# w_out in eight pieces, q of the first batch in whole rows, and 120 shifted priorities in a two-stage kernel that orders itself

## The chip, the cores and the metric

The kernel runs on one core of one Trainium2 chip. The metric is the device time of one execution in microseconds; the kernel before was run three times. A profile is one execution, with its own time.

## What is computed

Attention with random features on 8 batches of 8 heads, 576 tokens of 64 values each, followed by a feed-forward layer with a gate on the 4608 tokens that result. Cut to what matters:

```python
# stage 1, per batch and head; q, k, v: [8, 8, 576, 64], omega: [128, 64]
q_s, k_s = q / 64**0.25, k / 64**0.25
def phi(x):                              # [.., 576, 128]
    h = x @ omega.T - sum(x * x) / 2
    return exp(h - max(h)) / sqrt(128)   # the maximum over the 128 features
q_p, k_p = phi(q_s), phi(k_s)
kv = k_p.T @ v                           # [128, 64]
z = sum(k_p, over tokens)
attn = (q_p @ kv) / (q_p @ z + 1e-6)

# stage 2; x: [4608, 512] (batch and token, head and value), w_in: [512, 2048], w_out: [2048, 512]
h = x @ w_in
out = (h * clip(h + 3, 0, 6) / 6) @ w_out
```

Inputs and output are float32; the products run in bf16. Terms of phi(q) that are the same for all features of a token cancel in the quotient, so for q only the exponential of the projection is formed; for k each token's scale is the reciprocal of its largest exponential.

## The kernel before

**Tiling.** A batch has four pairs of heads (m = 0 to 3) and 576 tokens: 512 "main" tokens and 64 left over, which are set side by side for the two heads of a pair. Main tokens of one head lie in 128 partitions by 4. A "double" is 128 columns of a transposed tile: two heads' or two rows' 64 values. Every PSUM tile is one bank of eight (`ring`).

**Stage 1 of one batch** (`attention`, and inside it `pair`): k and q are transposed (names `Tk`, `Tq`; matmuls at L430, from batch 2 on DMA transposes), projected on omega (`K`, L652; `Q`, L669), and ScalarE takes the exponential (L658, L673). VectorE takes the maxima of k's features (L661, `mx`) and their reciprocals (`cc`), v is scaled by them (`vc`, L763; for the left tokens `vcl`, L692). `kv` (L776, L778) gathers the pair's product into one bank, a copy makes it bf16 (`kvz`), `num` (L804) multiplies it with q's exponentials, VectorE divides (L820, `xb`), and a transpose (`X`, L430 again) gives xT. The left tokens of all batches are gathered in xS and make a ninth block.

**Stage 2 of one block of 512 tokens**: `mm1` (L872; for block 0 `mm1_half`, L897) multiplies with w_in, 16 groups of 128 features; ScalarE and VectorE form the gate (L878, L880; L906, L908) into gT; `mm2` (L930) multiplies with w_out, 16 products into each of four tiles of 128 tokens; a copy and a store follow. Block 0 goes in two halves, A and B: for half A only 256 tokens of every head have to be through stage 1. Its mm2 tiles 0 and 1 need half A alone.

**Loads.** Batch 0's k, q and v come as float32 by the queues of SyncE (SP) and ScalarE, and are cast by engines. All weights, and k and q of later batches, are cast by the DMA itself and are issued by GpSimd (POOL); v stays float32. `FIRST` is the order of batch 0's loads: in the kernel before k, its left tokens, then `("q", 1)`, half A of q (`q_half(0)`: rows of tokens 0 to 255, four transfers of 128 KB in runs of 512 B), v, and `("q", 2)`, half B, which is issued when v's last transfer has landed (`QB_GATE`). `W_GATE` holds the four pieces of w_in back until half A's last transfer is in. Batch 1's k is issued when w_in's second piece is in, its q after the third, its v after the fourth; w_out after a transfer of batch 1's k; batch 2's loads after w_out's pieces 1, 2 and 3.

**What sets the order.** The program records every operation with its engine or engines, an estimated duration, what it reads and writes, and a priority (`prio`, mostly the batch or block in which it is due). `Prog.schedule` then plays the program through with those durations: each engine takes, among the operations that could start earliest, the one with the lowest priority; an operation with several possible engines goes to one of them; DMA queues share a modelled rate. What comes out is a fixed order for each engine, and `emit` writes it with the semaphore waits that the reads and writes need. On the chip each engine executes its list in that order. Where TensorE is idle in that play before 21 us, operations named `idle` (L467, `fill`) are put in: matmuls on a constant, whose results nobody reads.

Of the kernel before, what the change touches and what calls it, by code (L numbers as in the profile page):

```python
# [13 lines left out]
FIT = 0.1  # L14
IDLE_UNTIL = 21.0
EV0 = (("ACT","DVE"), ("ACT","DVE"), ("POOL","DVE"), {"k": ("POOL", "ACT", "DVE"), "q": ("POOL", "ACT","DVE")})


class Virt:
# [299 lines left out]
def _emit(nc, es, q, k, v, omega, w_in, w_out, out):  # L319
    B, H, S, D = q.shape  # L320
# [5 lines left out]
    NP = H // 2  # L326
# [5 lines left out]
    MAIN = 512  # L332
# [1 line left out]
    HALVES = [(0, 2), (2, 4)]  # L334
    SPLIT = 3
    LATE = 0.4
    FIRST = [("k", 1), ("k", 0), ("q", 1), ("v", 0), ("v", 1), ("q", 2), ("q", 0)]
    QB_GATE = [("v32", 1, 3)]
    REST = [("k", 1), ("k", 0), ("q", 1), ("q", 0), ("v", 0), ("v", 1)]
    W_GATE = [("q32", 1, 3, 0)] * 4  # L340
    alpha = float(D) ** -0.25
    PE_T, PE_X = 2, 2
    SPARE = 1
# [56 lines left out]
    G = Prog()  # L400
    op = G.op

    def mmt(n):
        return 0.003 + n / 2400.0
# [70 lines left out]
    def w_in_piece(i, gate):  # L475
# [3 lines left out]
           -8.6 + 0.05 * i, reads=gate, writes=[("wi", i)], group="dwi%d" % i, inc=16, lat=1.0, name="wi%d" % i,  # L479
           issue=0.85, packet=91.0)  # L480

    def w_out_piece(g, gate):
        op("POOL", 2.95, lambda E: E.dma_start(
            wo[:, 4 * g:4 * g + 4, :], w_out[512 * g:512 * g + 512, :].rearrange("(c p) e -> p c e", p=128)),
           -0.2 + 0.05 * g, reads=gate, writes=[("wo", g)], group="dwo%d" % g, inc=16, lat=1.0, name="wo%d" % g,
           issue=0.85, packet=91.0)

# [4 lines left out]
    def load(b, eng, gates):  # L492
        pb = b % 2
        halves = HALVES if b == 0 else [(0, NP)]
        turn_of = [0]

        def dma(part, dst, src, n, keys, gate, prio, run):
            cast = b > 0 and part[0] in "kq"
            e = "POOL" if cast else eng[turn_of[0]] if turn_of[0] < len(eng) else "SP"
            op(e, n * (0.74 if b == 0 else 0.8) * {1024: 1.0, 512: 1.1, 256: 1.5}[run] / 262144.0,  # L500
               lambda E: E.dma_start(dst, src), prio + 0.001 * turn_of[0], reads=gate + (free if cast else []), writes=keys,  # L501
               group="d" + part + ("c" if cast else "") + (str(pb) if b and part != "v" else ""), inc=16, lat=1.0,
               name="%s.%d" % (part, b), issue=0.85 if cast else 0.47, packet={1024: 50.0, 512: 36.0, 256: 18.0}[run])
            turn_of[0] += 1


        free = [("kb", 0, x) for x in range(NDC)] if b == 1 else []

        def landing(t, hh, m0, m1):

            if t == "v" or b == 0:
                return [(t + "32", hh, m) for m in range(m0, m1)]
            return [(t + "b", pb, 2 + 4 * m + 2 * hh + x) for m in range(m0, m1) for x in range(2)]

        base = {t: (b - 1) - {"k": 0.32, "q": 0.30, "v": 0.20}[t] if b else -9.5 for t in "kqv"}

        def mains(t, src, dst):
            for x, (m0, m1) in enumerate(halves):
                for hh in range(2):
                    first = 64 * hh if t != "q" else 0  # L520
                    d = dst[:].rearrange("p m (h r) d -> p m h (r d)", h=2) if t == "v" else mains_of(dst)
                    rows = src[b, 2 * m0 + hh:2 * m1 - 1 + hh:2, first:first + MAIN, :]
                    dma("%s%d%d" % (t, hh, x), d[:, m0:m1, hh, :], rows.rearrange("m (p r) d -> p m (r d)", r=4),
                        131072 * (m1 - m0), landing(t, hh, m0, m1), gates[t], base[t], 1024)

        def lefts_of(t, hh):
            return [(t + "b", pb, x, hh) for x in range(2)]

        def lefts(t, src, dst):
            if t == "q":  # L530
                for hh in range(2):
                    dma("ql%d" % hh, dst[64 * hh:64 * hh + 64, 0:NP, :],
                        src[b, hh:H:2, MAIN:S].rearrange("m s d -> s m d"), 65536, [("q32l", hh)] if b == 0 else lefts_of(t, hh),
                        gates[t], base[t], 256)
            else:
                sap = src[b].rearrange("(m h) s d -> m (h s) d", h=2)[:, MAIN:MAIN + 128, :]
                dma(t + "l", vl[pb][:, :, 0:D] if t == "v" else dst[:, 0:NP, :],
                    sap.rearrange("m x d -> x m d"), 131072, [("vl", pb)] if t == "v" else [("k32l", 0)] if b == 0 else lefts_of(t, 0),
                    gates[t], base[t], 256)

        def q_half(half):

            for m0, m1 in HALVES:
                for hh in range(2):
                    d = q32[:, NP:, :].rearrange("p (m h s r) d -> p m h s (r d)", h=2, s=2, r=2)
                    rows = q[0, 2 * m0 + hh:2 * m1 - 1 + hh:2, 256 * half:256 * half + 256, :]
                    dma("q%d%d%d" % (hh, m0, half), d[:, m0:m1, hh, half, :], rows.rearrange("m (p r) d -> p m (r d)", r=2),
                        65536 * (m1 - m0), [("q32", hh, m, half) for m in range(m0, m1)], QB_GATE if half else [], base["q"], 512)

        tensors = {"k": (k, KB[pb] if b else k32), "q": (q, QB[pb] if b else q32), "v": (v, v32)}  # L550
        for t, part in FIRST if b == 0 else REST:
            if t == "q" and b == 0 and part:
                q_half(part - 1)
            else:
                (mains if part else lefts)(t, *tensors[t])


    def attention(b):
# [10 lines left out]
        def main_keys(t, ms, hs=(0, 1)):  # L569
            return [(t + "32", hh, m) for m in ms for hh in hs]  # L570
# [45 lines left out]
        if b == 0:  # L616
# [7 lines left out]
            for s in range(2):  # L624
                for m0, m1 in HALVES:
                    nm = "%d%s" % (m0 // 2, "AB"[s])
                    dbl = every(m0, m1, s)
                    cast("q", nm, 512, pairs(qb)[:, 2 * m0:2 * m1, s, :], pairs(q32)[:, 2 * m0:2 * m1, s, :],
                         [k_ + (s,) for k_ in main_keys("q", range(m0, m1))], dbl, 0)
                    turns("q", nm, dbl, alts(qT, s, m0, m1), qb, 0)  # L630
            for t, src, cst, dst in (("k", k32, kb, kT), ("q", q32, qb, qT)):
                late = 0 if t == "k" else LATE
# [283 lines left out]
    def mm2(blk, tc):  # L916
# [5 lines left out]
        for ci, (c0, c1) in enumerate(cols):  # L922
            w = c1 - c0
            vo = Virt(ring)
            for g in range(4):
                t = (blk + 1) + (4 * tc + g + 0.5) / 16.0 + 0.5 * ci

                def e(E, g=g, vo=vo, c0=c0, c1=c1):
                    for f in range(4 * g, 4 * g + 4):
                        ins = E.matmul(ring.t[vo.slot][:, 0:c1 - c0], gT[gu][:, f, 128 * tc:128 * tc + 128], wo[:, f, c0:c1],  # L930
                                       start=(f == 0), stop=(f == NF - 1))
                    return ins

                op("PE", 4 * mmt(w), e, t, reads=[("gT", gu, f, tc // 2) for f in range(4 * g, 4 * g + 4)] +
                   [("wo", g)],
                   writes=[vo], alloc=[vo] if g == 0 else [], lat=0.25,
                   spare=(3 if tc > 1 else 0) if blk == 0 and g == 0 else 0, name="mm2.%d.%d" % (blk, tc))
            keys = [("osb", ou, x) for x in ((0, 1) if w == 512 else (ci,))]
            op(EV_O, both(w), evac(lambda c0=c0, c1=c1: osb[ou][:, c0:c1], lambda vo=vo, w=w: ring.t[vo.slot][:, 0:w]),
               t - 0.05, reads=[vo], writes=keys, name="oev.%d.%d" % (blk, tc))  # L940
            if blk < 8:
                rows = out[blk * S:blk * S + MAIN, :]
                dsts = [(0, 128, rows[256 * (tc // 2):256 * (tc // 2) + 256, :].rearrange("(p r) e -> r p e", r=2)[tc % 2] if blk == 0 else
                         rows.rearrange("(p r) e -> r p e", r=4)[tc])]
            else:
                dsts = [(64 * i, 64, out[(2 * tc + i) * S + MAIN:(2 * tc + i) * S + S, c0:c1]) for i in range(2)]
            for p0, np_, dst in dsts:
# [6 lines left out]
    for b in range(B):  # L954
        if b == 0:
            load(0, ("SP", "ACT", "SP", "ACT"), {t: [] for t in "kqv"})
            for i in range(len(WI)):
                w_in_piece(i, [W_GATE[i]])
        elif b == 1:
            load(1, (), {"k": [("wi", 1)], "q": [("wi", 2)], "v": [("wi", 3)]})  # L960
            for g, key in enumerate((("kb", 1, 16),)*4):
                w_out_piece(g, [key])
        elif b == 2:
            load(2, (), {"k": [("wo", 1)], "q": [("wo", 2)], "v": [("wo", 3)]})
        else:
            load(b, (), {"k": [("m1", b - 2, 6)], "q": [("m1", b - 2, 9)], "v": [("m1", b - 2, 15)]})
        if b == 0:
# [21 lines left out]

    G.by_path([o for o in G.ops if o.name == "mm1.0B.0"], -0.3, 0.02)  # L990
    G.by_path([o for o in G.ops if o.name == "mm1.0A.0"], -1.0, 0.02)
    G.schedule()
    engs = {"PE": nc.tensor, "ACT": nc.scalar, "DVE": nc.vector, "POOL": nc.gpsimd, "SP": nc.sync}
    blkx = es.enter_context(nc.Block())
# [35 lines left out]
```

The softmax here doesn't subtract the row's maximum and nothing guards it: scores larger than these inputs give would overflow.

## Time and profile before

| | us |
|---|---|
| median of three runs | 325.93 (325.68 to 326.29) |
| the profiled execution's own time | 325.93 |
| its span, first to last instruction | 324.1 |
| TensorE busy (share of the span) | 315.3 (97%) |
| VectorE, ScalarE, GpSimd busy | 211.3, 188.6, 75.1 |
| granted TensorE clock, mean | 0.999 |

Busy time of TensorE by stretch of the span, where what is missing is idle: 16.39 of the first 18.00 us, 21.66 of the 24.00 to 42, 15.74 of the 16.00 to 58, 41.74 of the 42.00 to 100. Matmuls overlap and their ends are modelled, so a busy stretch can hold small gaps, and the fill matmuls count as busy.

The first loads and the POOL queue, from the views of single transfers: k's last transfer (the left tokens) lands 4.4 us after its issue at 2.17; q's half A 4.1 to 4.3 us after issues from 2.68 to 4.25; v's last at 12.01; w_in's four pieces are issued from 8.69 to 11.88 and take 6.0 to 14.5 us; w_out's four are issued from 28.55 to 31.53 and take 10.1 to 15.4.

In the page, "L430" is the line of every TensorE transpose, so k, q and x are told apart by the tile after the arrow (`p<-ident,qb` is a transpose of q). A bracket after a row names the idle time of the engine before the row and whose end ended it.

### The profile page before, as it was taken

Reading aid. Unit: us, or ns where it says so; the run is one execution under the profiler, and the core shown is the slowest. Engines: PE = TensorE matmul, PEld = TensorE weight load, DVE = VectorE, ACT = ScalarE, POOL = GpSimd, SP = SyncE. Lnnn points to the kernel's source line nnn. Section 1 sums busy time; section 2 is a strip of 40 time slices with the busy share of each in tenths; the row PEclk is TensorE's granted clock in tenths of the full one; section 3 lists DMA queues with packets and bytes.
Section 4 is the critical chain, followed back from the end, with each engine's and each line's share of the span. In section 5 each row is a group of like instructions: output and inputs, shape, how many; then the busy total and the mean of one; then the engine's idle time right before and its main releaser. Section 6 shows DMA issues by size and latency. Waiting matters only on the chain.

```text
span 324.1 us, 5845 instructions
## 1 busy us (share of the span) xinstructions
PE 315.3 (97%) x2204; PEld 175.0 (54%) x2238; DVE 211.3 (65%) x465; ACT 188.6 (58%) x380; POOL 75.1 (23%) x107
## 2 busy tenths in 40 slices
PE   8988999999999999999999999999999999999996
PEld 6777966454654545555455555545555444444443
DVE  5968897687595946986777577755865354434411
ACT  3948885576495626974866477747774353443400
POOL 3855053054131600550324022402011000000000
PEclk9999999999999999999999999999999999999999
DMA  8999979999781999599889953999021201000024
GB/s 234 260 214 212 238 116 218 245 176 193 148 163 34 126 205 278 68 184 142 219 100 138 214 192 44 155 200 244 0 68 52 85 4 63 33 34 32 32 65 99
DMA packets 92620, 44.79 MB, mean 138 GB/s; under 512 B 58160, under 2 KB 88112, under 8 KB 92592
## 3 DMA queue, kind: packets, MB, share of 16 engines
q1 hardware_dynamic: 65376, 31.31, 42.5%
q0 software_dynamic: 26512, 12.46, 30.6%
q10 hardware_dynamic: 704, 0.66, 0.6%
q8 instruction: 18, 0.29, 0.4%
q14 instruction: 10, 0.08, 0.1%
HBM read 36.73 MB, written 9.44 MB: 142 GB/s over the span
## 4 chain that ended last, share of the span: by engine, by line
PE 87%; DMA 5%; ACT 3%; SPq 2%; issue 1%; DVE 1%
PE p L930 38%; PE p L872 32%; PE p L652 4%; PE p L669 4%; DMA q<-in_q_dram 3%; PE p L804 3%; PE p L897 3%; SPq L501 2%; PE p L776 2%; DMA v<-in_v_dram 2%; ACT qpT L673 1%; PE p L430 1%; ACT tsb L878 1%; ACT kp L658 1%; PE p L778 0%
## 5 line engine op out<-in xcount | busy, mean ns | idle before, releaser
L930 PE MATMUL p<-wo,gT 128*128 128x512 bf16 (+2 forms) x576 | 139.6, 373 | 0.9 <-issue 0.2
L880 DVE SCALAR_TENSOR_TENSOR gT<-tsb,p 128x512 bf16<-128x512 bf16 x128 | 86.8, 685 | 58.6 <-ACT tsb L878 57.3
L878 ACT ACTIVATE tsb<-p 128x512 bf16<-128x512 f32 x128 | 76.6, 601 | 74.2 <-PE p L872 73.2
L872 PE MATMUL p<-xT,wi 128*128 128x512 bf16 x434 | 105.6, 379 | 0.8
L930 PEld LDWEIGHTS p<-wo,gT 128*128 128x128 bf16 x592 | 56.1, 98 | 56.9
L872 PEld LDWEIGHTS p<-xT,wi 128*128 128x128 bf16 x448 | 42.7, 98 | 45.8
L661 DVE TENSOR_REDUCE mx<-kp 128x4 f32<-128x512 bf16 x72 | 47.0, 675 | 14.3 <-ACT kp L658 14.1
L658 ACT ACTIVATE kp<-p 128x512 bf16<-128x512 f32 x72 | 40.4, 610 | 14.3 <-PE p L652 14.3
L673 ACT ACTIVATE qpT<-p 128x512 bf16<-128x512 f32 (+1 forms) x80 | 41.1, 576 | 5.2 <-PE p L669 5.2
L763 POOL TENSOR_TENSOR vc<-v,cc 128x512 bf16<-128x512 f32 x20 | 21.5, 1073 | 29.8 <-DVE cc L759 23.5
L820 DVE TENSOR_TENSOR xb<-p,rec 128x384 bf16<-128x384 f32 (+1 forms) x64 | 28.3, 477 | 0.1
L652 PE MATMUL p<-om,kT 128*128 128x256 bf16 x144 | 23.2, 273 | 0.0
L669 PE MATMUL p<-qT,om 128*128 128x512 bf16 (+1 forms) x78 | 22.3, 357 | 0.0
L419 DVE COPY osb<-p 128x512 f32<-128x512 f32 (+2 forms) x12 | 7.8, 646 | 18.2 <-PE p L930 18.2
L418 ACT COPY osb<-p 128x512 f32<-128x512 f32 x25 | 14.7, 586 | 7.6 <-PE p L930 7.3
L652 PEld LDWEIGHTS p<-om,kT 128*128 128x128 bf16 x144 | 13.5, 98 | 9.6 <-ACT kT L418 0.2
L501 POOL DMA_DIRECT2D k<-in_k_dram x12 | 9.2, 771 | 39.7 <-PE p L669 26.9
L804 PEld LDWEIGHTS p<-kvz,qpT 128*128 128x128 bf16 x312 | 14.0, 98 | 6.5 <-ACT kvz L418 0.2
L897 PE MATMUL p<-xT,wi 128*128 128x256 bf16 x128 | 16.5, 273 | 0.5 <-DVE xT L419 0.4
L872 PE MATMUL p<-xS,wi 128*128 128x512 bf16 x62 | 16.2, 379 | 0.1
L804 PE MATMUL p<-kvz,qpT 128*128 128x65 bf16 x312 | 15.4, 194 | 0.0
L776 PEld LDWEIGHTS p<-vc,kp 128*128 128x128 bf16 x256 | 12.0, 98 | 6.1 <-DVE vc L763 0.6
(68 smaller groups left out, 216.2 us busy)
## 6 DMA issues: line engine op xcount, KB each, us to landing
out_dram<-osb SPq DMA_DIRECT2D x32, 256.0 KB, 3.2
v<-in_v_dram SPq DMA_DIRECT2D x14, 512.0 KB, 5.6
wi<-in_moe_w_in_dram POOLq DMA_DIRECT2D x4, 512.0 KB, 10.9
k<-in_k_dram POOLq DMA_DIRECT2D x8, 256.0 KB, 5.0
k<-in_q_dram POOLq DMA_DIRECT2D x8, 256.0 KB, 6.7
wo<-in_moe_w_out_dram POOLq DMA_DIRECT2D x4, 512.0 KB, 12.7
kb<-in_k_dram POOLq DMA_DIRECT2D x6, 256.0 KB, 5.0
qb<-in_q_dram POOLq DMA_DIRECT2D x6, 256.0 KB, 6.8
```

The lines of the kernel that those rows point to most:

```text
L652: ins = E.matmul(ring.t[vK.slot][:, 256 * i:256 * i + 256], kT[:, 2 * u + i, :], om[:].rearrange("d t m -> d (t m)"), start=True, stop=True)
L658: op("ACT", actt(512), lambda E, u=u, vK=vK: E.activation(kp[pb][:, 4 * u:4 * u + 4, :].rearrange("p c m -> p (c m)"), ring.t[vK.slot], AF ...
L661: op("DVE", dvet(512), lambda E, u=u: E.reduce_max(mx[pb][:, 4 * u:4 * u + 4], kp[pb][:, 4 * u:4 * u + 4, :], axis=AX.X), pos(u) + 0.03, r ...
L669: op("PE", mmt(n), lambda E, vQ=vQ, lh=lh: E.matmul(ring.t[vQ.slot][:, 0:n], om[:, lh, :], src, start=True, stop=True), p + 0.045 * lh, re ...
L673: op("ACT", actt(n), lambda E, vQ=vQ, lh=lh: E.activation(dst(lh), ring.t[vQ.slot][:, 0:n].rearrange("m (j t) -> m j t", t=128), AF.Exp, s ...
L804: ins = E.matmul(d[:, hh, i - i0, :], qpT[pb][:, o:o + 128], kvz[m][:, 65 * hh:65 * hh + 65], start=True, stop=True)
L820: op("DVE", dvet(128 * n), lambda E: E.tensor_tensor(xv(i0, i1), psum()[:, :, :, 0:64], rbc, ALU.mult), t + 0.01, reads=[vn, ("rec", ru)], ...
L872: ins = E.matmul(ring.t[vh.slot], wi[:, c, 128 * f:128 * f + 128], xv[:, c, :], start=(c == 0), stop=(c == NJ - 1))
L878: op("ACT", actt(512), lambda E: E.activation(tsb[tu][:], ring.t[vh.slot], AF.Relu, bias=0.5, scale=1.0 / 6.0), t - 0.1, reads=[vh], write ...
L880: op("DVE", dvet(512), lambda E: E.scalar_tensor_tensor(gT[gu][:, f, :], tsb[tu][:], 1.0, ring.t[vh.slot], ALU.min, ALU.mult), t - 0.1, re ...
L897: ins = E.matmul(ring.t[vh.slot][:, 256 * g:256 * g + 256], wi[:, c, 128 * (f + g):128 * (f + g) + 128], xT[0][:, c, 256 * half:256 * half ...
L930: ins = E.matmul(ring.t[vo.slot][:, 0:c1 - c0], gT[gu][:, f, 128 * tc:128 * tc + 128], wo[:, f, c0:c1], start=(f == 0), stop=(f == NF - 1))
```

## The change

Four things change.

- q of batch 0 is loaded whole: four transfers of 256 KB in runs of 1 KB, between k and v, as k and v are. `QB_GATE` and `q_half` go; the casts of half A and half B both read these four transfers (two each for pairs 0 and 1, two each for pairs 2 and 3), and the four pieces of w_in wait for the last of the four. A token's half is now its row within a run of four, so block 0's store uses the same pattern as all others.
- w_out is loaded in eight pieces of 256 rows in the place of four of 512. In block 0, mm2 is recorded in eight groups of two products per tile (before: four of four); the other blocks keep four groups.
- Batch 2's k, q and v wait for w_out's pieces 4, 5 and 7 of eight (before: 1, 2 and 3 of four).
- Before the order is made, 120 operations get their priority shifted by the amounts of a table (`NUDGE`); with these, the order of every engine is made anew.

Cut to its core:

```diff
+NUDGE = {
+    114: 0.0222, 119: 0.0169, 120: 0.0216, 122: 0.0313, 123: 0.0172, 124: -0.0176, 134: -0.0037, 137: 0.0668,
...
+    663: 0.0694, 664: -0.0408, 665: -0.013, 750: 0.1102, 763: 0.0243, 783: -0.019, 830: 0.0578,
+}
...
-    FIRST = [("k", 1), ("k", 0), ("q", 1), ("v", 0), ("v", 1), ("q", 2), ("q", 0)]
-    QB_GATE = [("v32", 1, 3)]
+    FIRST = [("k", 1), ("k", 0), ("q", 1), ("v", 0), ("v", 1), ("q", 0)]
...
-    W_GATE = [("q32", 1, 3, 0)] * 4
+    W_GATE = [("q32", 1, 3)] * 4
...
+    WO = [(2 * i, 2 * i + 2) for i in range(8)]
+
     def w_out_piece(g, gate):
-        op("POOL", 2.95, lambda E: E.dma_start(
-            wo[:, 4 * g:4 * g + 4, :], w_out[512 * g:512 * g + 512, :].rearrange("(c p) e -> p c e", p=128)),
+        f0, f1 = WO[g]
+        op("POOL", 0.7375 * (f1 - f0), lambda E: E.dma_start(
+            wo[:, f0:f1, :], w_out[128 * f0:128 * f1, :].rearrange("(c p) e -> p c e", p=128)),
...
-        def q_half(half):
-
-            for m0, m1 in HALVES:
-                for hh in range(2):
-                    d = q32[:, NP:, :].rearrange("p (m h s r) d -> p m h s (r d)", h=2, s=2, r=2)
-                    rows = q[0, 2 * m0 + hh:2 * m1 - 1 + hh:2, 256 * half:256 * half + 256, :]
-                    dma("q%d%d%d" % (hh, m0, half), d[:, m0:m1, hh, half, :], rows.rearrange("m (p r) d -> p m (r d)", r=2),
-                        65536 * (m1 - m0), [("q32", hh, m, half) for m in range(m0, m1)], QB_GATE if half else [], base["q"], 512)
...
-                         [k_ + (s,) for k_ in main_keys("q", range(m0, m1))], dbl, 0)
+                         main_keys("q", range(m0, m1)), dbl, 0)
...
-            for g in range(4):
-                t = (blk + 1) + (4 * tc + g + 0.5) / 16.0 + 0.5 * ci
+            for f0, f1 in WO if blk == 0 else [(4 * g, 4 * g + 4) for g in range(4)]:
+                g = f0 // 4
+                t = (blk + 1) + (4 * tc + f0 / 4.0 + 0.5) / 16.0 + 0.5 * ci
...
-            for g, key in enumerate((("kb", 1, 16),)*4):
+            for g, key in enumerate((("kb", 1, 16),) * len(WO)):
                 w_out_piece(g, [key])
         elif b == 2:
-            load(2, (), {"k": [("wo", 1)], "q": [("wo", 2)], "v": [("wo", 3)]})
+            load(2, (), {"k": [("wo", 4)], "q": [("wo", 5)], "v": [("wo", 7)]})
...
+    for i, x in NUDGE.items():
+        G.ops[i].prio += x
     G.schedule()
```

## The prediction

> **What bounds the kernel now.** I read the page's head and its part 1 first, then the matmul timeline from the start of the span, then the chain of waits, and last the timelines of the other engines and the landing times of the loads in the first 26 us.
>
> ```profile
> span 324.1 us, 5845 instructions
> PE 315.3 (97%) x2204; PEld 175.0 (54%) x2238; DVE 211.3 (65%) x465; ACT 188.6 (58%) x380; POOL 75.1 (23%) x107
> ```
>
> TensorE is busy all the time, by its modelled ends. But some of it is `fill`: matmuls on a constant that only keep the engine running. The timeline shows where they stand, and where real work waits:
>
> ```profile
> 9.56 3.22 PE L467 MATMUL p<-fill 128*128 128x256 bf16 x28
> ...
> 17.93 0.60 PE L897 MATMUL p<-xT,wi 128*128 128x256 bf16 x4
> ...
> 21.00 0.40 PE L430 MATMUL p<-ident,qb 128*128 128x128 bf16 x4 [0.70 <-POOL qb L419]
> ...
> 25.07 0.40 PE L430 MATMUL p<-ident,qb 128*128 128x128 bf16 x4 [1.16 <-ACT qb L418]
> ...
> 31.27 2.79 PE L897 MATMUL p<-xT,wi 128*128 128x256 bf16 x24 [0.39 <-DVE xT L419]
> ...
> 42.34 0.81 PE L930 MATMUL p<-wo,gT 128*128 128x512 bf16 x3 [0.15 <-issue]
> ```
>
> The first useful product of the second stage (L897) starts at 17.93 us; two transposes of q wait after it, and the first product with w_out (L930) starts at 42.34. The chain says whose fault the waits are, and how the run ends:
>
> ```profile
> 6.90 5.11 DMA v<-in_v_dram
> ...
> 13.48 10.90 DMA q<-in_q_dram
> ...
> 313.40 7.77 PE p L930 x51
> ```
>
> The second half of q is issued only when v has landed (12.01), takes 10.90 us for 128 KB beside w_in, and lands at 24.38. The last matmul ends at 321.17.
>
> Now the sum that carries everything. From rows of back-to-back work one matmul costs 0.216 us at 512 columns (24 in 5.18), 0.1085 at 256 (8 in 0.87), 0.056 per transpose (16 in 0.89), about 0.031 at 65 columns. By the code's counts there remain from 42.34 on: 576 products with w_out, of which the last 16 are each cut in two (124.4), 512 with w_in (110.6), 108 of K (11.7), 56 wide and 14 narrow of Q (13.6), 28 kv groups of 0.31 (8.7), 280 num products (8.7), 20 transposes (1.1). Sum 278.8; the trace has 321.17 - 42.34 = 278.83. So after 42.34 TensorE loses nothing measurable. Before 42.34 the useful work is 27.2 us (mm1 of block 0: 13.9; K of two batches 3.9; Q 1.95; kv 1.3; num 1.25; transposes and the rest 4.9). So 15.1 us are lost, all of them in the first 42. Only this can be won or lost, unless the new order breaks the saturated part.
>
> **What the Trainium skill says.** "DMA: Bandwidth & Descriptors", section Issuing engines are not separate DMA queues: all loads run on the same 16 DMA engines and interleave, whoever issues them. The trace agrees: the first half of q took 4.1 to 4.3 us per transfer, the second up to 10.9 beside w_in. Same page, section Why small descriptors are slow: each packet carries a fixed cost. The trace fits: q in runs of 512 B moved 0.5 MB between 6.57 (k's last landing) and 8.69 (first w_in issue, released by q), 247 GB/s; v in runs of 1 KB moved 1.18 MB from there to 12.01, 355 GB/s. "GPSIMD Engine Reference", section 1. Specifications: GpSimd shares its SBUF ports with VectorE when that reads two SBUF inputs. The trace agrees: the same scaling of v (L763) took 0.69 us on VectorE alone at 11.50 and 1.12 at 15.30 beside GpSimd's.
>
> **The change part by part.**
>
> *q in whole rows, ahead of v.* Four transfers of 256 KB in the place of four of 128 KB, and four issues of the SP queue after v are gone (2 us of queue time that nothing needs). 1 MB at 247 to 355 GB/s is 4.2 to 3.0 us from 6.57 on: q ends between 9.5 and 10.8; I take 9.9. v's two first transfers then land at about 11.8, its last at about 13.4, against 12.01. VectorE needs v first at 11.65 (behind five maxima of 0.61 and the reciprocals, as now at 11.50), so v's delay costs 0.2 there. The removed waits are the two on q's second half: gaps of 0.86 us (19.92 + 0.22 to 21.00) and 1.32 (23.62 + 0.13 to 25.07), together 2.2 us; 0.55 more before 31.27 was the same half's late xT.
>
> *w_in waits for all of q.* GpSimd starts its four issues at 9.9 and not 8.69; they take 3.19, so the work behind them on that engine moves too: one vcl 13.1 to 13.9, two vc (1.05 each) to about 16.0-16.3, a cast of q (0.62) to 16.9. ScalarE gets more in this stretch (a k cast and q's transposes before the last exponentials): eighteen pieces of 0.5 to 0.65 us in a row put its kvz copies at about 16 to 17. VectorE: four more maxima, a vcl of 0.43 to 0.87 (0.43 alone, 0.87 beside GpSimd's, from two rows of batch 1 and 2), the last vc to 17.5. With 0.2 us from a matmul's end to its reader (17.33 to 17.54 now), X of pair 0 comes at 18.3 and the first L897 at about 19.1, 1.2 later than now. But much of the second half's work of q (transposes, Q) is already done by then.
>
> *The order before the first w_out product.* In the built program's order `fill` stands 60 times against 65. The first 21 are the same and end at the same place (5.5 us lost with the start). The other 39 at 0.108 are 4.2 us, against 44 now, 4.8. Walking the order with the durations above: the sixteen fills before the first kv end near 14.4, the DVE half of vcl at 14.5, so kv of pair 0 runs at 14.55; Q of the next rows to 15.4, four fills, kv of pair 1 at 15.6; the first num at 16.1 (behind kvz on ScalarE), the second at 16.95 (its kvz likewise); kv of pairs 2 and 3 from 17.35 (GpSimd's vc) to 17.95; four transposes of q to 18.2; X 18.3; L897's first two parts at 19.1 and 19.5; X of pairs 2 and 3 and Q in turn with ScalarE's copies to 20.65; four-plus-four num products. TensorE so reaches the third part of the first L897 group at about 20.95 us, with 18.45 us of useful work left to the first w_out product (27.1 in all, 8.65 done; two narrow transposes fewer stand before it). From there I find nothing late: w_in's four pieces would have to be there at 18.9, 22.8, 24.8 and 26.5; now they land between 14.7 and 25.6, behind half of q that is now out of the way. VectorE's list from 22.9 to batch 1's last xT is 26 us, done by about 49, and TensorE wants it at 54. I allow 0.4 for small waits: first w_out product at 20.95 + 18.45 + 0.4 = 39.8, 2.5 earlier than 42.34. Bounds of this step: 38.9 (no wait in the walk from 15.8 on costs more than half of what I gave it) to 42.3 (q at 247 GB/s, +0.9; w_in's last piece 1.2 later than now, +0.6; VectorE's slow values, +1.0).
>
> *w_out in eight pieces.* The same bytes; four more issues of 0.76 us on GpSimd (3.0), hidden because that engine is idle 9.18 us there now. A piece of 256 rows can be used when half of a present piece has come. Now the first 512 rows land at 28.55 + 10.1 = 38.65 and the last at 46.2. A first quarter megabyte needed at 39.8 would be there near 37.4, the next at 38.65 (needed 40.9), the last at 46.2 (needed about 50.7). Without this split an earlier TensorE would have only 1.1 us in hand at the first piece; with it 2.4. Its own gain is nothing now; its cover, if gone, would cost up to 1 us. Matmuls and weight loads stay the same number. Gates of batch 2's loads move to pieces 4, 5 and 7, which land where pieces 2 and 3 did.
>
> *The shifted priorities later.* TensorE's order differs through batch 5. Everything after 39.8 remains 278.8 if no operand is late. I looked at the three tight places: K of batch 2 now stands two groups of w_in later (about 68, 66.7 now), so its DMA transposes have the same time; K of batch 3 at 85 to 87 follows a transpose that SP must issue behind a v load gated by block 1's last L872 (about 74), 6.3 us to land, 6 in hand; nine K products of batch 4 nearly in a row hold ScalarE for 4.6 us against 4.5 of TensorE work. I take 0 for this step, 1.5 at most.
>
> Sum, against the profiled execution's own time of 325.93 (span 324.1; 1.8 lies around it): 325.93 - 2.5 = 323.4. That execution's time is the median of the three runs, so no correction.
>
> **Rivals.** (1) *The stall moves.* The q waits go, but the later start of L897 and the w_in pieces give it back: the front at its slow values, first w_out product at 42.0, 325.6. For it: w_in starts 1.2 later, and GpSimd, VectorE and ScalarE are all full from 10 to 16. Against: the second half of q no longer stands between w_in's bytes. (2) *The whole front slides with q*, the slower side. Place: the landing of q's last transfer, which gates both w_in and, by the SP queue, v. Each microsecond there moves GpSimd's issues, vcl, vc, X and the first L897 by one, and w_in, batch 1's k and q and w_out behind it on the same queue. Price: (landing - 9.9) - 2.5. It decides from 12.4 on; at 13.6 the time is 327.1. For it: the page's first two slices moved 234 and 260 GB/s, less than I count on. Against: even 247 gives 10.8. (3) *More is won*: waits of the walk overlap, 38.9, 322.5.
>
> **How the numbers follow.** Forecast 0.60 (323.4), more won 0.08 (322.5), the stall moves 0.15 (325.6), the slide or a stall that the new order makes in the saturated part 0.17 (327.1). What a measurement can tell from no change is about 0.2% (0.65 us): faster is below 325.3, slower above 326.6. Faster: 0.60 + 0.08 + a little of the third, 0.70; within 0.2%: 0.13; slower 0.17. The range 322.3 to 326.7 takes in the bounds of the front (38.9 to 42.3) with the 1.5 of the saturated part on part of them, and leaves out most of the slide.
>
> **What would show it.** Right: no wait of L430 on a cast of q; first L897 near 19.1, first L930 near 39.8; 278.8 us from there to the last matmul (now 278.83); q's last landing near 9.9; all w_in before 26. Wrong: a first L930 at 42 or later, or more than 280 us from it to the last matmul; waits of L897 on w_in; of L930 on w_out; of L652 or L669 on a DMA transpose.

## The result, and the profile after

The changed kernel took 322.82 us as a median of four runs (322.39 to 323.25), beside 325.89 for the kernel before (four runs, 325.68 to 326.29): a ratio of 0.9904, interval [0.9885, 0.9923]. That is 3.1 us less, where 2.5 was forecast. The profiled execution took 323.14, with a span of 321.2. The lines of the code have moved: L897, L930, L430, L652, L669, L763, L692 and L804 of before are now L907, L941, L449, L662, L679, L773, L702 and L814.

The head of the page of the changed kernel (the columns as before):

```profile
span 321.2 us, 5834 instructions
PE 313.5 (98%) x2198; PEld 173.8 (54%) x2233; DVE 208.2 (65%) x459; ACT 190.2 (59%) x384; POOL 80.1 (25%) x113
```

TensorE is still busy nearly all the time, and the span is 2.9 us shorter. As fill counts as busy, this line does not tell what was won. The timeline of TensorE's matmuls in the same execution shows where:

```profile
12.32 1.91 PE L486 MATMUL p<-fill 128*128 128x256 bf16 x16
14.87 0.43 PE L786 MATMUL p<-vc,kp 128*128 128x65 bf16 x8 [0.64 <-DVE vcl L702]
...
18.03 0.39 PE L449 MATMUL p<-ident,qb 128*128 128x128 bf16 x4
...
19.06 0.66 PE L907 MATMUL p<-xT,wi 128*128 128x256 bf16 x4
...
20.61 1.04 PE L907 MATMUL p<-xT,wi 128*128 128x256 bf16 x8
...
39.28 0.81 PE L941 MATMUL p<-wo,gT 128*128 128x512 bf16 x3
```

The transposes of q at 18.03 have no bracket, nor has a later one: both waits on q's late half (0.70 and 1.16 us) are gone. The first L907 comes 1.1 us later than before (19.06 against 17.93), and yet the first product with w_out 3.06 earlier (39.28 against 42.34). The last matmul ends at 318.22 (the chain's end, below), so 278.94 us lie between; before it was 278.83. Everything that was won was won before 39 us. The view of waits of the same kernel, for TensorE (engine, tile and line that waits, whose end it waits for, us in total, times, longest):

```profile
PE p L486 <- DVE fill L481: 1.3, 1, 1.3
PE p L449 <- POOL kb L438: 0.7, 1, 0.7
PE p L786 <- DVE vcl L702: 0.6, 1, 0.6
```

Three waits are left. None of them is on q, on w_in, on w_out or on xT. The last two are new; the one on a cast of k lies ahead of all this, in the start of the kernel. Where the one on `vcl` comes from is in the chain of waits of the changed kernel:

```profile
6.69 5.66 DMA v<-in_v_dram
...
12.43 0.13 DVE vc L773
...
13.09 1.27 DVE mx L671 x2
...
14.39 0.44 DVE vcl L702
...
14.87 0.43 PE p L786 x8
...
313.69 4.54 PE p L941 x36
```

The front now hangs on v, not on q's second half: v's first pairs land at 12.35 behind all of q, VectorE scales them, forms two maxima that stand next in its list, and only then the small product `vcl` that the first kv needs.

### The profile page after: what moved, and what is told of

Same layout as the page of the kernel before. It is cut to its first block, busy times and chain, and to the rows that moved or that the text cites. A ratio compares the mean times of both kernels' runs of the same rounds, so it can differ in the third digit from the quotient of the medians.

```text
span 321.2 us, 5834 instructions
## 1 busy us (share of the span) xinstructions
PE 313.5 (98%) x2198; PEld 173.8 (54%) x2233; DVE 208.2 (65%) x459; ACT 190.2 (59%) x384; POOL 80.1 (25%) x113
## 4 chain that ended last, share of the span: by engine, by line
PE 92%; DMA 2%; SPq 2%; ACT 2%; issue 1%; DVE 1%; DVEq 0%; ACTq 0%
PE p L941 38%; PE p L882 33%; PE p L907 4%; PE p L662 4%; PE p L679 4%; PE p L814 3%; PE p L786 2%; DMA v<-in_v_dram 2%; SPq L523 2%; PE p L449 1%; ACT qpT L683 1%; ACT tsb L888 1%; PE p L788 1%; DVE mx L671 0%; DVE gT L890 0%
## 5 line engine op out<-in xcount | busy, mean ns | idle before, releaser
L941 PE MATMUL p<-wo,gT 128*128 128x512 bf16 (+2 forms) x574 | 138.7, 373 | 0.9
L941 PEld LDWEIGHTS p<-wo,gT 128*128 128x128 bf16 x592 | 56.3, 98 | 58.0
L668 ACT ACTIVATE kp<-p 128x512 bf16<-128x512 f32 x72 | 39.7, 610 | 17.5 <-PE p L662 17.4
L773 POOL TENSOR_TENSOR vc<-v,cc 128x512 bf16<-128x512 f32 x23 | 24.3, 1055 | 35.4 <-DVE cc L769 26.1
L662 PE MATMUL p<-om,kT 128*128 128x256 bf16 x144 | 22.5, 273 | 0.0
L679 PE MATMUL p<-qT,om 128*128 128x512 bf16 (+1 forms) x76 | 22.0, 357 | 0.1
L662 PEld LDWEIGHTS p<-om,kT 128*128 128x128 bf16 x144 | 13.5, 98 | 7.2
L702 POOL TENSOR_TENSOR vcl<-vl,cc 64x260 bf16<-64x260 f32 x8 | 5.0, 620 | 49.4 <-DVE cc L698 49.2
L814 PEld LDWEIGHTS p<-kvz,qpT 128*128 128x128 bf16 x312 | 13.8, 98 | 6.2 <-ACT kvz L437 0.3
L907 PE MATMUL p<-xT,wi 128*128 128x256 bf16 x128 | 15.8, 273 | 0.0
L814 PE MATMUL p<-kvz,qpT 128*128 128x65 bf16 x312 | 15.0, 194 | 0.1
```

The source lines that it names most:

```text
L662: ins = E.matmul(ring.t[vK.slot][:, 256 * i:256 * i + 256], kT[:, 2 * u + i, :], om[:].rearrange("d t m -> d (t m)"), start=True, stop=True)
L668: op("ACT", actt(512), lambda E, u=u, vK=vK: E.activation(kp[pb][:, 4 * u:4 * u + 4, :].rearrange("p c m -> p (c m)"), ring.t[vK.slot], AF ...
L679: op("PE", mmt(n), lambda E, vQ=vQ, lh=lh: E.matmul(ring.t[vQ.slot][:, 0:n], om[:, lh, :], src, start=True, stop=True), p + 0.045 * lh, re ...
L814: ins = E.matmul(d[:, hh, i - i0, :], qpT[pb][:, o:o + 128], kvz[m][:, 65 * hh:65 * hh + 65], start=True, stop=True)
L907: ins = E.matmul(ring.t[vh.slot][:, 256 * g:256 * g + 256], wi[:, c, 128 * (f + g):128 * (f + g) + 128], xT[0][:, c, 256 * half:256 * half ...
```

## The experiments

Twelve runs: seven edits, the changed kernel itself twice, and three of the edits a second time or turned round. Runs 1 to 4, 5 to 8, and 9 to 12 are three groups, each measured beside the kernel before (326.17, 326.28 and 326.48 us as medians).

The last column of the table separates kernels whose medians do not. The first loads land at different times from one execution to the next: the first issue of w_in, which GpSimd makes some 0.3 us after q's last landing, stands anywhere from 9.81 to 11.21 us in the twelve profiled executions in which it waits for all of q, though the order of the loads up to there is the same. All that follows moves with it. So the last column is the end of the last matmul less that issue. The spread is older than q: it is there when k's last transfer lands. That transfer is issued at about 2.17 us in all of them and takes from 4.3 us (run 8) to 5.7 (run 1). Two of them, from the lists of DMA issues (KB, us from issue to landing), first in the profiled execution of the changed kernel,

```profile
k<-in_k_dram SPq DMA_DIRECT2D x1, 128.0 KB, 5.0
```

and in run 3:

```profile
k<-in_k_dram SPq DMA_DIRECT2D x1, 128.0 KB, 4.4
```

From that landing to w_in's first issue it is 3.3 to 3.4 us in all twelve.

| kernel | median, us | ratio to before, interval | w_in issue | first kv | last matmul | less w_in issue |
|---|---|---|---|---|---|---|
| changed | 322.82 | 0.9904 [0.9885, 0.9923] | 10.58 | 14.87 | 318.22 | 307.64 |
| changed, run 5 | 322.76 | 0.9906 [0.9873, 0.9938] | 10.21 | 14.50 | 317.85 | 307.64 |
| changed, run 9 | 323.21 | 0.9893 [0.9877, 0.9909] | 10.92 | 15.22 | 318.56 | 307.64 |
| 1 no shifts | 324.13 | 0.9925 [0.9907, 0.9942] | 11.21 | 15.50 | 319.54 | 308.33 |
| 2 q whole only | 323.96 | 0.9928 [0.9916, 0.994] | 10.30 | 14.59 | 318.95 | 308.65 |
| 3 w_out tied in pairs | 323.08 | 0.9902 [0.9887, 0.9916] | 9.97 | 15.26 | 318.61 | 308.64 |
| 4 before, no gate on q | 324.90 | 0.9956 [0.9945, 0.9968] | 8.89 | 13.47 | 320.11 | 311.22 |
| 6 early shifts | 324.15 | 0.993 [0.9907, 0.9953] | 10.00 | 14.29 | 318.07 | 308.07 |
| 10 early shifts again | 323.83 | 0.9914 [0.99, 0.9929] | 10.31 | 14.61 | 318.22 | 307.91 |
| 11 late shifts | 323.58 | 0.9912 [0.9895, 0.9929] | 9.88 | 15.18 | 319.19 | 309.31 |
| 7 fewer fills | 324.16 | 0.9922 [0.9903, 0.9941] | 10.01 | 14.31 | 318.52 | 308.51 |
| 8 VectorE's order | 322.47 | 0.9876 [0.9858, 0.9894] | 9.81 | 13.70 | 317.07 | 307.26 |
| 12 VectorE's order again | 322.19 | 0.9869 [0.9854, 0.9883] | 10.20 | 14.09 | 317.45 | 307.25 |

The kernel before has 321.17 - 8.69 = 312.48 in the last column, but its w_in waits for half of q only. Three executions of the changed kernel give 307.64 each time. From the first w_out product to the last matmul all of them need 278.8 to 279.4 us. The record of the very first of these products is missing from every trace but those of runs 9 to 12, as three stand in a row where those runs show four; that is 0.22 us, and such differences between these figures mean nothing.

**1. The changed kernel without the shifts.**

```diff
-    for i, x in NUDGE.items():
-        G.ops[i].prio += x
     G.schedule()
```

> The changed kernel with the table of shifted priorities left out (q whole, w_out in eight pieces; every order made anew). Theory Q (the loss of the kernel before is the wait for q's second half, and loading q whole removes it): about 323.5 us, between 322.9 and 324.2; first product with w_out at 39.5 to 40.5 us, no transpose of q waiting on a cast after 18 us. Theory P (the shifted priorities are what brings the gain): 325 us or more, and the waits come back elsewhere before the first product with w_out.

324.13 us, inside theory Q's bounds, at their upper end, and 1.3 above the changed kernel's median. q's waits are gone here too; TensorE waits 0.44 us for `vcl` and 0.73 for a `vc`, and the first w_out product stands at 40.36. But q landed late in this execution (w_in's issue at 11.21). Counted from there it is 308.33 against 307.64: the shifts are worth 0.7 us in the trace.

**2. q whole alone: no shifts, w_out in four pieces.**

```diff
-    WO = [(2 * i, 2 * i + 2) for i in range(8)]
+    WO = [(4 * i, 4 * i + 4) for i in range(4)]
...
-            load(2, (), {"k": [("wo", 4)], "q": [("wo", 5)], "v": [("wo", 7)]})
+            load(2, (), {"k": [("wo", 1)], "q": [("wo", 2)], "v": [("wo", 3)]})
...
-    for i, x in NUDGE.items():
-        G.ops[i].prio += x
```

> The changed kernel with neither shifted priorities nor eight pieces: q whole, w_out in four pieces of 512 rows. Theory Q: within 0.4 us of the run without the table, because the first piece of w_out lands near 38.5 us and is needed about 40. Theory W (the finer pieces let the first products with w_out start earlier): at least 0.8 us slower than the run without the table, with a wait of the w_out products on a w_out transfer.

323.96 us, 2.2 below the kernel before beside it; first w_out product at 40.15, and no wait for w_out. So q in whole rows, with w_in held back behind all of it, does most of the work by itself. Against run 1, which has the eight pieces, the medians differ by 0.17 the one way and the traces by 0.32 the other: not told apart.

**3. The changed kernel's own order, but each product with an even piece of w_out also waits for the next.** The first product then needs 512 rows, as before the change.

```diff
     G.schedule()
+    piece = {o.name: o for o in G.ops}
+    for o in G.ops:
+        if o.name.startswith("mm2.0."):
+            for g in range(0, 8, 2):
+                if piece["wo%d" % g] in o.deps:
+                    o.deps[piece["wo%d" % (g + 1)]] = True
```

> The changed kernel in exactly its own order, but each product of block 0 that uses an even piece of w_out also waits for the odd piece after it, so that w_out is of use only in steps of 512 rows. Theory Q: no change, 322.8 us within 0.4, since the second piece lands at about 38.3 and the first product stands at 39.28. Theory W: 0.8 to 1.5 us slower, with waits on w_out.

323.08 us, within the changed kernel's 322.8 to 323.2, and no wait for w_out. The eight pieces bring nothing that this order needs. Yet the last column is 1.00 more than the changed kernel's, with nothing of w_out in it: the first kv comes 5.29 us after w_in's issue, not 4.29. VectorE's timeline of this kernel shows the reason,

```profile
11.81 0.89 DVE L773 TENSOR_TENSOR vc<-v,cc 128x512 bf16<-128x512 f32 x1 [0.28 <-DVE cc L769]
...
13.91 1.30 DVE L702 TENSOR_TENSOR vcl<-vl,cc 64x260 bf16<-64x260 f32 x1
```

and GpSimd's timeline of the same kernel its other half:

```profile
9.97 3.18 POOL L496 DMA_DIRECT2D wi<-in_moe_w_in_dram  x4 [0.52 <-DMA q<-in_q_dram]
13.13 0.67 POOL L702 TENSOR_TENSOR vcl<-vl,cc 64x260 bf16<-64x260 f32 x1
13.88 1.04 POOL L773 TENSOR_TENSOR vc<-v,cc 128x512 bf16<-128x512 f32 x1
```

GpSimd's `vc` began at 13.88, VectorE's `vcl` at 13.91, and the latter took 1.30 us: it ended 0.29 after GpSimd's. In the changed kernel's own execution the order of the two starts is the other way round. VectorE's timeline:

```profile
12.43 0.74 DVE L773 TENSOR_TENSOR vc<-v,cc 128x512 bf16<-128x512 f32 x1 [1.03 <-DMA v<-in_v_dram]
...
14.39 0.43 DVE L702 TENSOR_TENSOR vcl<-vl,cc 64x260 bf16<-64x260 f32 x1
```

GpSimd's timeline:

```profile
10.58 3.18 POOL L496 DMA_DIRECT2D wi<-in_moe_w_in_dram  x4 [0.51 <-DMA q<-in_q_dram]
13.75 0.66 POOL L702 TENSOR_TENSOR vcl<-vl,cc 64x260 bf16<-64x260 f32 x1
14.49 2.35 POOL L773 TENSOR_TENSOR vc<-v,cc 128x512 bf16<-128x512 f32 x2
```

VectorE was first by 0.10 us (14.39 against 14.49) and needed 0.43; GpSimd's two `vc` then took 2.35 together, not 2 x 1.05. "SBUF — State Buffer", section Who interferes with whom, of the Trainium skill says that the pair of ports which the two engines share is an exclusive lock, that the order of issue decides who blocks, and that a VectorE instruction with two inputs in SBUF contends with a GpSimd instruction that reads SBUF. These rows agree with it, nearly to the end: the blocked `vcl` ended 0.29 after GpSimd's `vc`, which is 0.14 less than its own 0.43. The changed kernel thus stands 0.1 us from a loss of 1.0 us, and which side it falls on varies: run 3 has the changed kernel's order and fell on the other one, and so did run 11 below. What made VectorE late there is its first `vc`, which took 0.89 us in run 3 and 1.05 in run 11 in the place of 0.74; why it did is not shown.

**4. The kernel before, in its own order, without the gate that holds q's second half back behind v.** This is the change's gain without any of its moves.

```diff
     G.schedule()
+    for o in G.ops:
+        if o.name in ("q001.0", "q101.0", "q021.0", "q121.0"):
+            o.deps = {d: raw for d, raw in o.deps.items() if not d.name.startswith("v")}
```

> The kernel before in exactly its own order, but q's second half is issued behind v without waiting for v to land (the region it writes has no earlier reader). Theory Q: the two waits of q's transposes (0.86 and 1.32 us) and the one behind them (0.55) go, 322.9 to 324.0 us; first product with w_out near 39.9. Rival: the transfers only share the same bandwidth with w_in, so that q's second half still lands after 20 us or w_in lands later by as much, 325.3 us or more.

324.90 us, 1.3 below before: less than the one theory and more than the other expected. The waits on q are gone. TensorE's timeline of this kernel (its lines are those of before) has another in their place:

```profile
20.55 0.39 PE L897 MATMUL p<-xT,wi 128*128 128x256 bf16 x2 [1.30 <-DMA wi<-in_moe_w_in_dram]
...
41.27 0.81 PE L930 MATMUL p<-wo,gT 128*128 128x512 bf16 x3 [0.15 <-issue]
```

The same bytes of q now run beside w_in's first pieces. Those take 8.2 us at the least and 11.7 in the middle, where they took 6.0 and 10.9 before, and 1.30 us of the 2.2 come back as a wait for w_in. In run 2, where w_in waits for all of q, there is no such wait. Run 2 also moves q in runs of 1 KB and not 512 B and has another order, so how much of the 0.9 us between the two runs belongs to each is not shown. The longer runs do carry more: between 6 and 8 us all loads together moved 279 GB/s in the kernel before and 282 in run 4, against 336 to 362 in the kernels with q in whole rows.

**5. The changed kernel again.**

> The changed kernel itself once more, beside the next three on the same chip: 322.8 to 323.1 us, ratio 0.990 to 0.991.

322.76 us; w_in's issue at 10.21 instead of 10.58, every later row earlier by the same 0.37, and 307.64 again.

**6. The early shifts alone.** By the table these are 56 of the 120.

```diff
     for i, x in NUDGE.items():
-        G.ops[i].prio += x
+        if i < 256 or 403 <= i <= 431:
+            G.ops[i].prio += x
```

> The changed kernel with the shifts of batch 0's operations and of half A of block 0's first product alone (the first 254 numbers and 403 to 431); all later operations keep their own priorities. The order up to the end of half A is the changed kernel's. Theory F (the priorities bring their 1.1 us only by the front, before the first useful L907): the changed kernel's time within 0.4 us. Theory L (the later shifts matter too): 323.6 us or more.

324.15 us, which is theory L's number, with runs from 322.87 to 325.0; but the interval overlaps the changed kernel's. Unclear, and therefore taken up again in run 10.

**7. The changed kernel's order without the last 39 fills** (what they waited for is handed to what waited for them).

```diff
     G.schedule()
+    fills = [o for o in G.order if o.name == "idle"][21:]
+    for r in fills:
+        for o in G.order:
+            if r in o.deps:
+                del o.deps[r]
+                for d, raw in r.deps.items():
+                    o.deps[d] = o.deps.get(d, False) or raw
+    G.order = [o for o in G.order if o not in set(fills)]
```

> The changed kernel's own order without the last 39 fill matmuls (results that nobody reads), so that TensorE idles there. If fills only stand where a wait would be: within 0.3 us of the changed kernel. If they hold the clock up: 0.5 to 2 us slower, with a granted clock under 1 between 12 and 20 us. If they stand in the way: up to 0.5 us faster.

This leaves out matmuls whose results nobody reads. 324.16 us, 1.4 above run 5, though the two intervals overlap; 0.87 more in the last column, all of it between the first kv and the third part of L907 (6.60 us against 5.74). TensorE's timeline of this kernel shows how long it then stands still, soon after another pause of 0.87,

```profile
10.82 0.40 PE L449 MATMUL p<-ident,qb 128*128 128x128 bf16 x4 [0.87 <-ACT qb L437]
...
14.31 0.43 PE L786 MATMUL p<-vc,kp 128*128 128x65 bf16 x8 [2.40 <-DVE vcl L702]
```

and its busy time by stretch what follows (stretch, its length, busy us and instructions of PE, PEld, DVE, ACT and POOL, granted clock, share of the DMA engines, GB/s):

```profile
14.00:16.00 2.00, 1.69 (x24) 1.18 (x24) 1.93 (x6) 1.25 (x5) 1.92 (x2) 0.82 1.22 201
16.00:18.00 2.00, 1.71 (x25) 1.31 (x23) 1.71 (x6) 1.03 (x4) 1.64 (x3) 0.50 1.24 206
18.00:20.00 2.00, 2.00 (x31) 1.69 (x28) 1.05 (x5) 1.68 (x6) 0.58 (x1) 0.82 1.24 208
```

The clock falls to 0.50 after the gap. A mean of 0.82 over 2 us is 0.72 us at half clock (0.18 x 2 / 0.5), so it lasts 0.72 + 2 + 0.72 = 3.4 us. In the changed kernel it is 1.00 in these stretches. "TensorE: Matmul & The Clock Gate", Part 1 of the Trainium skill, puts the window by which the clock is set at about 3.4 us; the length agrees. It has half clock come after at least one idle window of that length; here shorter pauses were enough. So in this execution the fills earn about 0.9 us by what they keep up; nothing was lost by them in front of a wait, since the first kv comes 4.30 us after w_in's issue with them and without. In three of the six executions the mean clock is 0.989 and not 0.995, by the same sum some 7 us at half clock (an estimate: 0.011 x 322 / 0.5). No profile was taken of one of these, so what they lost by it is open.

**8. The changed kernel with VectorE's `vcl`, and one maximum, ahead of its first `vc`.**

```diff
     G.schedule()
+    vc0 = next(o for o in G.order if o.name == "vc.0.0")
+    vcl0 = next(o for o in G.order if o.name == "vcl.0" and o.eng == "DVE")
+    mx5 = next(o for o in G.order if o.name == "mx0.5")
+    G.order = [o for o in G.order if o is not vc0 and o is not vcl0]
+    at = G.order.index(mx5)
+    G.order[at:at + 1] = [vcl0, mx5, vc0]
```

> The changed kernel's own order except on VectorE, where the left tokens' scaling (vcl) and one maximum go ahead of the first scaling of v, which waits 1.03 us for v to land; nothing is left out. If VectorE's list from 11.4 us on is what sets the front: kv of pair 0 at about 14.45 in place of 14.87, the first L907 0.4 to 0.8 us earlier, 322.1 to 322.5 us. If GpSimd's list or ScalarE's sets it: no change within 0.3 us.

322.47 us. That lies in the range of the first theory, and the first kv comes 3.89 us after w_in's issue, not 4.29; but the interval overlaps run 5's, so run 12 repeats it.

**9. The changed kernel once more, beside the next three.**

> The changed kernel again, as the yardstick of this call: 322.2 to 323.2 us as a median, ratio near 0.990. Theory that its executions differ because the first loads land at different times: first product with w_out between 38.9 and 39.7, 278.8 to 279.0 us from there to the last matmul.

323.21 us with w_in's issue late, at 10.92, and 307.64 in the last column.

**10. The early shifts again** (edit as in run 6).

> The early shifts alone, again (55 of the 120: batch 0, and the first products of block 0's half A). Theory A, the later shifts bring nothing: median within 0.5 us of the changed kernel's in this call. Theory B, they bring about 1 us: median 0.8 to 1.5 above it, as 324.15 against 322.76 was; then the stretch from the first product with w_out to the last matmul must be longer than 278.9 by that much in most executions (a span more than 0.8 longer at the same start).

323.83 us, 0.6 above run 9: between the two theories. The trace is clearer: 307.91, and 308.07 in run 6, against 307.64. So the later shifts bring 0.3 to 0.4 us. What the early ones do can be seen too: from the first kv to the first w_out product it is 24.41 us in the changed kernel and in run 6, and 24.86 in run 1. Without them (runs 1, 2 and 11) TensorE waits 0.73 us for a `vc` of VectorE; with them that wait is gone. The medians say more than that, 0.6 and 1.4, and the profile does not show why: the spans of the five runs here have a median of 321.3, those of run 9 of 321.4, but up to 3.0 us of a run's time lie outside its span here, where run 9 has 1.8. That stays open.

**11. The other 64 shifts alone** (edit against run 6).

```diff
-        if i < 256 or 403 <= i <= 431:
+        if not (i < 256 or 403 <= i <= 431):
```

> The other 65 shifts alone (batch 1 and later, block 0's half B on). Theory A: no gain beyond no shifts at all, 324.0 to 324.4, first product with w_out near 40.3. Theory B: about 323.2 to 323.6, through fewer waits after 42 us. If it is slower than no shifts at all, the two sets belong together.

323.58 us, theory B's number, but with an interval that overlaps those of no shifts and of early shifts. In the trace it is 309.31; 1.01 of that is VectorE's `vcl` losing to GpSimd (it took 1.13 us, first kv 5.30 after w_in's issue, as in run 3). If all of that reaches the end, as the 1.00 of run 3 did, 308.30 are left without it, the 308.33 of no shifts at all. So the trace shows no gain of the later shifts alone; the medians cannot decide it.

**12. VectorE's order again** (edit as in run 8).

> The changed kernel with two short operations of VectorE ahead of the first vc, again. Theory that this takes 0.3 to 0.4 us off the front: median 0.3 to 0.5 below the changed kernel's in this call, first product with w_out 38.1 to 38.9 depending on the landings. Rival, the first time was luck of the landings: median within 0.2 of the changed kernel's, or above.

322.19 us, 1.0 below the changed kernel of run 9; the intervals of the ratio, [0.9854, 0.9883] and [0.9877, 0.9909], still touch. The trace repeats itself: the first kv 3.89 us after w_in's issue in both runs, against 4.29 or 4.30 in three executions of the changed kernel, and 307.25 in the last column, 0.39 less. VectorE's timeline of this run:

```profile
11.11 0.43 DVE L702 TENSOR_TENSOR vcl<-vl,cc 64x260 bf16<-64x260 f32 x1
11.55 0.69 DVE L671 TENSOR_REDUCE mx<-kp 128x4 f32<-128x512 bf16 x1
12.16 0.68 DVE L773 TENSOR_TENSOR vc<-v,cc 128x512 bf16<-128x512 f32 x1
```

The two operations lie in the time in which VectorE waited 1.03 us for v; `vc` has no bracket any more. And `vcl` is done before GpSimd has left its DMA issues, so the race of run 3 is no longer run. This kernel has the lowest median in each of its two groups; 0.4 us of its lead are shown, more is not.

## Why the prediction was right, and where its sizes were off

- **What bounds it.** Right. The transposes of q wait no more, the first L907 stands at 19.06 (19.1 foretold), and 278.94 us of the changed kernel lie behind the first w_out product (278.8 foretold); in every run it is 278.8 to 279.4. Only the front could pay for the change as a whole.
- **q whole, ahead of v.** Right in its mechanism: both waits on q went, and run 2 shows 2.2 us from this part without the shifts and the eight pieces. That the two gaps also summed to 2.2 is not a proof that they are the same 2.2: the first L907 came later and the order changed as well.
- **Where q lands.** w_in's first issue was put at 9.9 and stood at 10.58, 0.68 later; q's last landing, put at the same 9.9, came at about 10.3 (issued at 4.26, 6.0 us on its way). The mis-sized term is where the sum starts, not the rate: "from 6.57 on" is k's last landing in the kernel before, and in this execution k landed at about 7.2 (issued at 2.17, 5.0 on its way). From k's landing to w_in's issue 3.33 were foretold, and 3.3 to 3.4 are measured in all twelve executions; in run 3, where k landed at 6.57 again, the issue stood at 9.97. The two rates were read up to w_in's issue at 8.69 and not to q's landing at 8.35 (4.25 + 4.1), so they are rough, and the "9.5 to 10.8" worked out with them fit the landings of twelve executions by luck: these moved with k's landing. v followed as foretold: `vc` starts 1.85 us after w_in's issue (1.95 foretold). That VectorE waited 1.03 for it and not 0.2 is the same delay again, and VectorE being ready at 11.40.
- **The order before the first w_out product.** Too long by 1.2 us, which more than paid for the 0.68. From w_in's issue to the first kv 4.65 were foretold and 4.29 measured; VectorE's `vcl` took 0.43, the low end of what was allowed. From that kv to the third part of L907 6.40 were foretold and 5.74 measured: kv of pairs 2 and 3 came at 2.53 and not 2.8 behind the first, X at 3.39 and not 3.75, and the two small L907 parts and what lies between took 1.55, not 1.85. From there to the first w_out product 18.85 were foretold, the 0.4 for small waits among them, and 18.67 measured. Sum 0.36 + 0.66 + 0.18 = 1.20, less 0.68: 39.28 in the place of 39.8. That the first L907 came so close to 19.1 is luck: it was 0.68 late with the loads and early by 0.36 at the first kv and 0.36 more at X.
- **VectorE's `vcl`, "0.43 to 0.87".** Wrong as a bound. It was read as a slowing by shared ports; it is a block nearly to the end of GpSimd's instruction, and runs 3 and 11 show 1.30 and 1.13. The changed kernel's profiled execution fell on the good side by 0.1 us.
- **w_out in eight pieces at nothing.** Right: run 3 needs no more time, and no wait for w_out appears in it or in run 2, whose first w_out products stand at 39.67 and 40.15.
- **The later shifts at nothing.** Nearly: 0.3 to 0.4 us by the traces of runs 6 and 10, won behind the first w_out product (278.94 us with them, 279.37 in run 6), and none by themselves in the trace of run 11. What the prediction did not have is a price for the early shifts apart from q. All shifts together make 0.69 (308.33 less 307.64), so the early ones, too, make 0.3 to 0.4.
- **The rivals.** "The stall moves" is a real mechanism, but for another edit: in run 4 the half of q beside w_in gives 1.30 us back. In the changed kernel nothing waits for w_in on TensorE. "The whole front slides with q" would have decided at a landing of 12.4; the latest w_in issue seen was 11.21. "More is won" (38.9 and 322.5 us, at a chance of 0.08) came closer than the forecast (39.8 and 323.4) to the first w_out product, 39.28, and to the median, 322.82; the forecast was closer to the profiled execution's 323.14. Its reason held as well: the walk's allowances were too wide.

## What to carry to other kernels

If a saturated stretch has the same length in two kernels, take its start as the result and look only at what lies before it; and before two profiled fronts are compared, subtract the landing that both of them hang on, which here moved by 1.4 us from run to run and hid differences of 0.4. Look for the earliest landing that moves: here it was k's, ahead of the transfer that the change was about. A late transfer is mended only in part by issuing it earlier if it then runs beside the one that is needed next (1.3 us in run 4, against 2.2 in run 2, which orders the two). Put a short VectorE operation that reads two SBUF operands before GpSimd's tensor work and not against it, above all if there is a wait for a load that it can fill.

## What the runs showed of the hardware

- A VectorE product of 64 x 260 took 0.43 us when it started 0.10 before a GpSimd product, and 1.30 when it started 0.03 after one (run 3), ending 0.29 after that one's end. In run 11 it took 1.13 when it started 0.20 after, ending 0.28 after that one's end. GpSimd paid when it was second: the two `vc` took 2.35 us, each 1.05 alone.
- Two pauses of TensorE, of 0.87 and 2.40 us with some 1.1 us between them, were enough for half clock, and that lasted 3.4 us (run 7), longer than either pause.
- With the same loads in the same order, w_in's first issue, which follows q's last landing, moved over 1.4 us between executions, with k's last landing, which it followed 3.3 to 3.4 us later each time. v's first pair followed it at a distance that stayed within 0.03 us (VectorE's `vc` started 1.83 to 1.86 us after that issue in the seven executions in which it waited for v).
